# One VectorE addition at the end of a batch: step 2 of the block, or left to steps 6 and 7

## The chip, the cores and the metric

The kernel runs on one core of one Trainium2 chip. The metric is the device time of one execution in microseconds (us), lower is better. A timed result is the median of several executions; each execution also reports the mean clock that TensorE was granted, as a share of full speed.

Names of the engines: PE is TensorE (PEld its weight loads), DVE is VectorE, ACT is ScalarE, POOL is GpSimd. The whole span of a trace is 1.7 to 1.9 us shorter than the device time of the same execution.

## The reference, cut to what matters

```python
B, N, C = 4, 6208, 256
# attention over channels, one softmax matrix a (256 x 256) for each batch
qn = q / (norm(q over the N tokens) + 1e-6);  kn = the same of k
a = softmax(kn.T @ qn / tau)
x = v @ a
# channel mix of x with its own previous row
xk = mu_k * x + (1 - mu_k) * x_prev;  xr = mu_r * x + (1 - mu_r) * x_prev
out = sigmoid(xr @ w_r) * (relu(xk @ w_k) ** 2 @ w_v)      # d_ff = 1024
```

The matrix `a` of a batch needs sums over all its 6208 rows: the products k.T @ q (on PE) and the sums of squares of q and k. Only then can the rows of that batch go through the channel mix.

## The kernel before

Batch 0's sums are made first. Then come blocks `i` of 512 rows, 12 to a batch, each in 8 steps `j`. While the blocks of one batch run, the sums of the next batch are made in the gaps ("units"). So there are three batch ends inside the loop, of batches 1, 2 and 3. The first is at about 130 us.

The sums of squares: ScalarE squares 128 x 1024 elements into a tile, and an entry is put in the list `adds`. VectorE later adds the tile into `acc`, at steps that the loop chooses:

```python
def unit_square(b, g, s):
    ...
    elif (g, s) == (1, 0):
        t = pn.tile([P, 2, 2 * C], F32, name="acc", tag="acc", bufs=2)
        sums[b] = t                       # the first squares go straight into acc
    else:
        t = pq.tile([P, 2, 2 * C], F32, name="sq2", tag=f"f{s // 2}", bufs=6)
        adds.append((now[0] + 2, b, t))   # to be added two steps later at the earliest
    ...
def next_add():
    _, b, t = adds.pop(0)
    nc.vector.tensor_tensor(sums[b], sums[b], t, op=OP.add)          # L230
```

At a batch's end a chain of small pieces makes `a`, one piece a step. `fold` adds the two halves of the sums and waits until none of this batch's additions is left:

```python
return [evac, fold, None, None, norms, roots, pow2, None, invert, None, None,
        turn, exp, shares, None, weigh]
...
FOLD = 15
for i in ...:
    for j in range(8):
        ...                               # finish(): res of a finished part
        if chain:
            piece = chain[0]
            if len(chain) == FOLD and any(e[1] == holds[0] for e in adds):
                piece = None              # fold waits for the last addition
            else:
                chain.pop(0)
            if piece is not None:
                piece()
        ...                               # up(), square(), down(), mix(): the block's work
        if j in slots and pos["mm"] < len(units):
            unit()
        if adds and adds[0][0] <= now[0] and (j in (1, 6, 7)
                or j == 2 and adds[0][1] == holds[0] and chain):      # L766
            next_add()
        now[0] += 1
```

The block's work, as far as the argument needs it. `up` makes kT_ps on PE (L494), and ScalarE takes it out as `kr` (L499). `square` makes `kk = kr * kr` on VectorE (L512). `down` multiplies xr with w_r (L527) and kk with w_v (L531) into vr_ps on PE. vr_ps has two buffers; ScalarE (L540) and VectorE (L541) read it out into `res`, and the next L527 has to wait for that. kr has two buffers too.

Of the kernel before, what the change touches and what calls it, by code (L numbers as in the profile page):

```python
# [18 lines left out]
def kernel(  # L19
# [61 lines left out]
    adds = []  # L81
    sums = {}
    now = [0]
# [262 lines left out]
    def v_load(i):  # L346
        b, t = blocks[i]
        v_bf = p2.tile([P, S, C], BF16, name="v_bf", tag="v_bf", bufs=6)
        nc.gpsimd.dma_start(v_bf, v[b, t * M:(t + 1) * M, :].rearrange("(s p) c -> p s c", p=P))  # L349
        st[i, "v"] = v_bf  # L350
# [66 lines left out]
    def mix_first(key, a, dh):  # L417

        c = slice(a * H, (a + 1) * H)
        m = less[:, dh:dh + 1] if key == "xk" else less[:, 2 + dh:3 + dh]  # L420
        nc.vector.scalar_tensor_tensor(st[0, key][:, dh, c], st[0, "ps"][a][1][:, dh], m,
                                       st[0, "x"][:, dh, a * H + 1:(a + 1) * H + 1], op0=OP.mult, op1=OP.add)

    def up_first(fh, a):

        c = slice(a * H, (a + 1) * H)
        if (fh, a) == (0, 0):
            st[0, "kk"] = p2.tile([P, 8, M], BF16, name="kk", tag="kk", bufs=2)
            st[0, "kr", 0] = p2.tile([P, 4, M], BF16, name="kr", tag="kr", bufs=2)
        if a == 0:  # L430
            st[0, "kT", fh] = ps.tile([P, M], F32, name="kT_ps", tag="kT_ps", bufs=3)
        kT_ps = st[0, "kT", fh][:, c]
        for dh in range(2):
            nc.tensor.matmul(kT_ps, w_k_sb[:, dh, fh * P:(fh + 1) * P], st[0, "xk"][:, dh, c],
                             start=dh == 0, stop=dh == 1)
        nc.scalar.activation(st[0, "kr", 0][:, fh, c], kT_ps, AF.Relu, scale=0.5 ** 0.5)
# [50 lines left out]
    def up(i, fh):  # L487
        m = size(i)
        if fh == 0:
            st[i, "kk"] = p2.tile([P, 8, M], BF16, name="kk", tag="kk", bufs=2)  # L490
        xk = st[i, "xk"]
        kT_ps = ps.tile([P, M], F32, name="kT_ps", tag="kT_ps", bufs=3)
        for dh in range(2):
            nc.tensor.matmul(kT_ps[:, :m], w_k_sb[:, dh, fh * P:(fh + 1) * P], xk[:, dh, :m],  # L494
                             start=dh == 0, stop=dh == 1)
        if fh % 4 == 0 and (i or fh):
            st[i, "kr", fh // 4] = p2.tile([P, 4, M], BF16, name="kr", tag="kr", bufs=2)
        kr = st[i, "kr", fh // 4][:, fh % 4, :m]
        nc.scalar.activation(kr, kT_ps[:, :m], AF.Relu, scale=0.5 ** 0.5)  # L499
        if fh == 0 and by_act(i):  # L500
            nc.scalar.activation(st[i, "kk"][:, 0, :m], kr, AF.Square)
# [4 lines left out]
    def square(i, fh):  # L506
        m = size(i)
        n = 4 if fh < 4 and i < NBLK - 1 else 2
        if fh % n == n - 1:
            lo = 1 if fh == 3 and by_act(i) else fh % 4 + 1 - n  # L510
            kr = st[i, "kr", fh // 4][:, lo:fh % 4 + 1, :m]
            nc.vector.tensor_tensor(st[i, "kk"][:, fh // 4 * 4 + lo:fh + 1, :m], kr, kr, op=OP.mult)  # L512

    def down(i, j):

        s, h = divmod(j, 2)
        if s * P >= size(i) or i == NBLK - 1:
            return
        kk = st[i, "kk"]
        if j == 0:  # L520
            st[i, "res"] = p2.tile([P, S, D], F32, name="res", tag="res", bufs=3)
        if h == 0:
            vr_ps = ps.tile([P, 2 * D], F32, name="vr_ps", tag="vr_ps", bufs=2)
            st[i, "vr"] = vr_ps
            xr = st[i, "xr"]
            for dh in range(2):
                nc.tensor.matmul(vr_ps[:, D:], xr[:, dh, s * P:(s + 1) * P], w_r_sb[:, dh, :],  # L527
                                 start=dh == 0, stop=dh == 1)
        vr_ps = st[i, "vr"]
        for fh in (range(3) if h == 0 else range(3, 8)):  # L530
            nc.tensor.matmul(vr_ps[:, :D], kk[:, fh, s * P:(s + 1) * P], w_v_sb[:, fh, :],  # L531
                             start=fh == 0, stop=fh == 7)

    def finish(i, s):
        if i == NBLK - 1:
            return
        res = st[i, "res"]
        vr_ps = st[i, "vr"]

        nc.scalar.activation(res[:, s], vr_ps[:, D:], AF.Tanh, scale=0.5)  # L540
        nc.vector.scalar_tensor_tensor(res[:, s], res[:, s], 1.0, vr_ps[:, :D], op0=OP.add, op1=OP.mult)  # L541
        b, t = blocks[i]
        dst = out[b, t * M:(t + 1) * M, :].rearrange("(s p) c -> p s c", p=P)
        if i < NBLK - 2:
            if s == S - 1:
                nc.sync.dma_start(dst, res)
        elif s % 2:

            nc.sync.dma_start(dst[:, s - 1:s + 1], res[:, s - 1:s + 1])
# [82 lines left out]
    chain = []  # L632
    FOLD = 15
    holds = [0]
# [60 lines left out]
    for i in range(-2, NBLK - 1):  # L695
        for j in range(8):
            if j % 2:
                if j == 1 and i >= 1:
                    finish(i - 1, 3)
                elif j > 1 and i >= 0:  # L700
                    finish(i, j // 2 - 1)
            if j == 0 and 4 <= i + 6 < NBLK - 1:
                v_load(i + 6)
# [3 lines that stand above are left out]
                    piece = None  # L707
# [4 lines that stand above are left out]
            if i == -1 and j < 3:  # L712
                for fh, a in (((0, 0), (1, 0), (0, 1)), ((1, 1),), ())[j]:
                    up_first(fh, a)
                if j == 2:
                    up(0, 2)
            elif 0 <= i + 1 < NBLK:
                up(i + 1, j)
            if i >= 0:
                if j == 0 :  # L720
                    square(i, 7)
            if j > 0 and 0 <= i + 1 < NBLK:
                square(i + 1, j - 1)
            if j > 0 and i >= 0:
                down(i, j - 1)
            elif j == 0 and i >= 1:
                down(i - 1, 7)
            if 0 < i + 2 < NBLK:
                n = i + 2
                full = 0 < n < NBLK - 1  # L730
                if j in (0, 2) and full:
                    x_half(n, int(j > 0))
                if j == 3:
                    mix_delta(n)
                if j in (4, 5):
                    mix(n, "xk", int(j > 4))

            if j in (0, 2) and i == -1:
                for a in range(2):
                    mix_first("xr", a, int(j > 0))  # L740
            elif j in (0, 2) and 0 <= i + 1 < NBLK:
                mix(i + 1, "xr", int(j > 0))
            if (i, j) in ((-1, 6), (0, 4)):
                v_transpose_pe(i + 3, nc.vector.tensor_copy)()
            if j == 5 and 4 <= i + 5 < NBLK - 1:
                v_transpose(i + 5)
            if i == -1 and j in (5, 6):
                for u in early[:2] if j == 5 else early[2:]:
                    unit_matmul(*u)
            if (i, j) in ((0, 1), (0, 3)):  # L750
                unit_square(*early[j - 1])
            if i < 0:
                slots = ()
            elif i == 0:
                slots = (5, 6, 7)
            elif i < 7:
                slots = (1, 2, 3, 4, 5, 7) if i < 3 else (1, 2, 3, 4, 5, 6, 7)
            elif i == 7:
                slots = (1, 2, 7)
            elif (i - 7) % NB == 0:  # L760
                slots = (5, 7)
            else:
                slots = (1, 3, 4, 5, 7) if (i - 7) % NB in (1, 3, 6, 9) else (1, 3, 5, 7)
            if j in slots and pos["mm"] < len(units):
                unit()
            if adds and adds[0][0] <= now[0] and (j in (1, 6, 7) or j == 2 and adds[0][1] == holds[0] and chain):  # L766
                next_add()
            now[0] += 1
            if i >= 0 and i % NB == 2 and j == 1 and i // NB < B:
                left_go[0] = left_x(i // NB)  # L770
            if i >= 0 and i % NB == 4 and j == 4 and i // NB < B:
                left_go[0][0]()
            if i >= 0 and i % NB == 6 and j == 4 and i // NB < B:
                left_go[0][1]()
# [36 lines left out]
```

## Time and profile before

| | before |
|---|---|
| device time, median of 3 (range) | 511.45 us (511.42 to 511.74) |
| PE busy | 485.9 of 510.2 us, 95% |
| VectorE busy | 444.0 us, 87% |
| ScalarE busy | 446.3 us, 87% |
| the 69 additions into acc | 84.2 us, 1.220 us each |

The profile is that of a further execution, which took 512.12 us with a granted clock of 0.997.

The page of before, its first part (busy time and instructions of each engine), and from its fifth part the group of the additions:

```profile
PE 485.9 (95%) x3441; PEld 331.3 (65%) x3441; DVE 444.0 (87%) x751; ACT 446.3 (87%) x925; POOL 99.9 (20%) x146
...
L230 DVE TENSOR_TENSOR acc<-acc,sq 128x1024 f32<-128x1024 f32 x69 | 84.2, 1220 | 0.0
```

The 1.220 us of an addition agree with the Trainium skill, "VectorE: DVE Perf Modes", section "The TRN2 errata — SBUF-src ops pay a fixed extra latency per instruction": its formula (N + 151) / 0.96 ns for an fp32 tensor_tensor addition gives an estimate of 1224 ns at N = 1024. What counts for a busy queue is another number. From the start of an addition to the start of the next VectorE instruction the trace has 1.135 us, for the middle eight tenths of the 69 within 1 ns. Reported spans overlap a little, so this text adds up starts, not spans.

The waits of before (engine and line, what it waited for; us in total, times, longest):

```profile
PE vT_ps L365 <- DMA v_bf<-in_v_dram: 1.5, 1, 1.5
...
PE vr_ps L527 <- DVE res L541: 1.2, 2, 0.8
PEld L531 <- DVE kk L512: 1.1, 5, 0.3
```

After the start-up (some 45 us, in which it waits far more) PE waits little, and the wait of L527 for `res` is the one that the change aims at. Before's stretches show where it lies (length, then busy time of each engine with its number of instructions):

```profile
core 0: us, PE busy (x) PEld busy (x) DVE busy (x) ACT busy (x) POOL busy (x), PEclk, DMA share, GB/s
...
118.00:128.00 10.00, 10.00 (x77) 6.98 (x75) 9.50 (x16) 9.97 (x23) 2.52 (x4) 1.00 1.31 215
128.00:138.00 10.00, 8.82 (x66) 5.66 (x65) 10.00 (x15) 8.69 (x19) 0.00 (x0) 1.00 1.35 204
138.00:148.00 10.00, 10.00 (x75) 7.22 (x74) 9.93 (x19) 9.02 (x20) 3.36 (x4) 1.00 1.01 169
```

Of these stretches only in that from 128 to 138 us is PE not busy all the time, and there VectorE is busy all the time: at the first batch end the kernel is bound by VectorE for some 10 us. PE's timeline of before there (start, length, instruction, number of them, and in brackets the idle time ahead of it):

```profile
129.79 0.59 PE L494 MATMUL kT_ps<-xk,w_k_sb 128*128 128x512 bf16 x2
131.21 0.38 PE L527 MATMUL vr_ps<-w_r_sb,xr 128*128 128x256 bf16 x2 [0.83 <-DVE res L541]
...
133.67 0.38 PE L527 MATMUL vr_ps<-w_r_sb,xr 128*128 128x256 bf16 x2 [0.35 <-DVE res L541]
```

The brackets subtract a modelled end, which makes a wait look too short. By starts: the second of the two 512-column matmuls of 129.79 starts at 130.00, and the next matmul starts at 131.21, 1.21 us later. At full rate it would be 0.22 us later. PE has lost 0.99 us. That rate is the Trainium skill's, "TensorE: Matmul & The Clock Gate", section "Wait — 56ns, not 53.3ns?": N / 2.4 GHz plus about 2.5 ns, 216 ns for 512 columns; this trace agrees, with a pair of such matmuls every 0.43 us. In the same way before loses 0.51 us at 133.67, 0.13 at 136.40 and 0.09 at 148.61: together 1.72 us.

VectorE's timeline of before shows who is in the way:

```profile
129.61 1.22 DVE L230 TENSOR_TENSOR acc<-acc,sq 128x1024 f32<-128x1024 f32 x1
130.74 0.41 DVE L541 SCALAR_TENSOR_TENSOR res<-res,vr_ps 128x256 f32<-128x256 f32 x1
131.07 0.69 DVE L469 TENSOR_TENSOR delta<-xT 128x1024 bf16<-128x1024 bf16 x1
...
147.87 0.69 DVE L512 TENSOR_TENSOR kk<-kr 128x1024 bf16<-128x1024 bf16 x1
...
151.57 0.95 DVE L512 TENSOR_TENSOR kk<-kr 128x1536 bf16<-128x1536 bf16 x1
```

The addition of 129.61 is the one of step 2. It stands right ahead of the `res` of 130.74, for which PE waits.

### The profile page before, as it was taken

The numbers are of one execution on the slowest core, as the hardware profiler recorded it, in microseconds if no ns is written. First come the engines' busy times: TensorE is split into PE (matmuls) and PEld (weight loads), VectorE is DVE, ScalarE is ACT, GpSimd is POOL, SyncE is SP. The second block draws the span as 40 slices with busy tenths as digits, with TensorE's granted clock in tenths as the row PEclk, the third lists the DMA queues.
The fourth block names the chain that finished last, engine by engine and source line by source line (L and its number), as shares of the span: only waits on it lengthen the run. The fifth ranks groups of instructions, "written<-read, shape, count | busy, mean of one in ns | idle before, by whom it ended". The sixth has DMA issues, their size and how long they took to land. (4 is left out here: it accounts for less than half of the span.)

```text
span 510.2 us, 9336 instructions
## 1 busy us (share of the span) xinstructions
PE 485.9 (95%) x3441; PEld 331.3 (65%) x3441; DVE 444.0 (87%) x751; ACT 446.3 (87%) x925; POOL 99.9 (20%) x146
## 2 busy tenths in 40 slices
PE   4678999999999999999999999999999999999996
PEld 1345666766567677676666767667666666666675
DVE  3776899999999999999979999999878787878884
ACT  5767999999899999999899999999897888888784
POOL 0044342223054132221243133000131100000000
PEclk9998999999999999999999999999999999999999
DMA  8999999999989999997599999924497763333123
GB/s 330 409 299 201 191 173 199 143 192 199 201 153 198 180 205 172 171 184 134 102 157 227 173 173 177 176 74 116 84 178 137 143 106 97 93 85 83 45 81 104
DMA packets 133462, 83.46 MB, mean 164 GB/s; under 512 B 50660, under 2 KB 126760, under 8 KB 133416
## 3 DMA queue, kind: packets, MB, share of 16 engines
q0 software_dynamic: 56592, 33.01, 50.1%
q1 hardware_dynamic: 76504, 49.59, 41.1%
q8 instruction: 27, 0.44, 0.4%
q10 hardware_dynamic: 320, 0.26, 0.2%
q14 instruction: 19, 0.16, 0.1%
HBM read 78.71 MB, written 25.43 MB: 204 GB/s over the span
## 5 line engine op out<-in xcount | busy, mean ns | idle before, releaser
L499 ACT ACTIVATE kr<-kT_ps 128x512 bf16<-128x512 f32 (+1 forms) x390 | 232.0, 606 | 27.8 <-PE kT_ps L494 24.0
L531 PE MATMUL vr_ps<-w_v_sb,kk 128*128 128x256 bf16 x1536 | 231.0, 273 | 0.1
L494 PE MATMUL kT_ps<-xk,w_k_sb 128*128 128x512 bf16 (+1 forms) x780 | 230.0, 377 | 0.2 <-DVE xk L479 0.2
L531 PEld LDWEIGHTS <-kk 128*128 128x128 bf16 x1536 | 149.5, 98 | 58.9 <-DVE kk L512 1.1
L541 DVE SCALAR_TENSOR_TENSOR res<-res,vr_ps 128x256 f32<-128x256 f32 x192 | 80.1, 417 | 42.8 <-ACT res L540 42.8
L512 DVE TENSOR_TENSOR kk<-kr 128x1536 bf16<-128x1536 bf16 (+2 forms) x148 | 117.1, 791 | 0.2 <-ACT kr L499 0.2
L494 PEld LDWEIGHTS <-w_k_sb 128*128 128x128 bf16 x780 | 75.5, 98 | 27.5 <-issue 0.6
L230 DVE TENSOR_TENSOR acc<-acc,sq 128x1024 f32<-128x1024 f32 x69 | 84.2, 1220 | 0.0
L540 ACT ACTIVATE res<-vr_ps 128x256 f32<-128x256 f32 x192 | 76.5, 398 | 1.3 <-PE vr_ps L531 1.3
L527 PE MATMUL vr_ps<-w_r_sb,xr 128*128 128x256 bf16 x384 | 73.3, 272 | 1.2 <-DVE res L541 1.2
L479 DVE SCALAR_TENSOR_TENSOR xr<-delta,mu_t,xT 128x512 bf16<-128x512 bf16 x94 | 70.1, 746 | 0.0
L479 DVE SCALAR_TENSOR_TENSOR xk<-delta,mu_t,xT 128x512 bf16<-128x512 bf16 x94 | 70.1, 746 | 0.0
L527 PEld LDWEIGHTS <-xr 128*128 128x128 bf16 x384 | 37.6, 98 | 46.4 <-issue 2.6
L388 ACT CAST xT<-xT_ps 128x512 bf16<-128x512 f32 x94 | 55.4, 589 | 12.1 <-PE xT_ps L386 11.9
L386 PE MATMUL xT_ps<-vT,a_sb 128*128 128x512 bf16 x188 | 55.9, 379 | 0.9 <-DVE vT L371 0.8
L242 PE MATMUL s_ps<-qk 128*128 128x256 bf16 (+1 forms) x294 | 55.8, 273 | 0.0
L127 POOL DMA_DIRECT2D qk<-in_q_dram x39 | 26.2, 672 | 136.6 <-ACT kr L499 53.3
L226 ACT ACTIVATE sq<-qk 128x1024 f32<-128x1024 bf16 (+1 forms) x49 | 51.0, 1041 | 0.0
L349 POOL DMA_DIRECT2D v_bf<-in_v_dram x48 | 37.1, 776 | 50.7 <-DMA vT<-v_bf 32.4
L190 PE MATMUL s_ps<-qk 128*128 128x384 bf16 (+2 forms) x98 | 20.3, 352 | 16.0 <-ACT qk L147 14.9
L469 DVE TENSOR_TENSOR delta<-xT 128x1024 bf16<-128x1024 bf16 x47 | 32.3, 686 | 1.1 <-ACT xT L388 1.1
L242 PEld LDWEIGHTS <-qk 128*128 128x128 bf16 (+1 forms) x294 | 28.5, 98 | 5.6 <-issue 0.8
(105 smaller groups left out, 242.1 us busy)
## 6 DMA issues: line engine op xcount, KB each, us to landing
out_dram<-res SPq DMA_DIRECT2D x47, 512.0 KB, 4.2
v_bf<-in_v_dram POOLq DMA_DIRECT2D x48, 256.0 KB, 9.0
qk<-in_q_dram POOLq DMA_DIRECT2D x36, 256.0 KB, 8.0
qk<-in_k_dram POOLq DMA_DIRECT2D x36, 256.0 KB, 8.8
f<-in_q_dram SPq DMA_DIRECT2D x11, 512.0 KB, 9.4
f<-in_k_dram SPq DMA_DIRECT2D x11, 512.0 KB, 9.9
vT<-v_bf SPq DMA_TRANSPOSE x44, 6.7
f<-in_q_dram SPq DMA_DIRECT2D x2, 256.0 KB, 9.0
```

What stands on the lines that cost most here:

```text
L230: nc.vector.tensor_tensor(sums[b], sums[b], t, op=OP.add)
L242: nc.tensor.matmul(s_ps[:, ih, :], rows_at(qk, b, g, 0)[:rows, s, ih * P:(ih + 1) * P], rows_at(qk, b, g, 1)[:rows, s, :], start=t0 and ih ...
L386: nc.tensor.matmul(xT_ps, a_sb[:, b, ih, dh * P:(dh + 1) * P], vT[:, :, ih, :], start=ih == 0, stop=ih == 1)
L388: nc.scalar.copy(xT[:, dh, 1:], xT_ps)
L479: nc.vector.scalar_tensor_tensor(o[:, dh], st[i, "d"][:, dh], mu[:, dh:dh + 1], st[i, "x"][:, dh, :M], op0=OP.mult, op1=OP.add)
L494: nc.tensor.matmul(kT_ps[:, :m], w_k_sb[:, dh, fh * P:(fh + 1) * P], xk[:, dh, :m], start=dh == 0, stop=dh == 1)
L499: nc.scalar.activation(kr, kT_ps[:, :m], AF.Relu, scale=0.5 ** 0.5)
L512: nc.vector.tensor_tensor(st[i, "kk"][:, fh // 4 * 4 + lo:fh + 1, :m], kr, kr, op=OP.mult)
L527: nc.tensor.matmul(vr_ps[:, D:], xr[:, dh, s * P:(s + 1) * P], w_r_sb[:, dh, :], start=dh == 0, stop=dh == 1)
L531: nc.tensor.matmul(vr_ps[:, :D], kk[:, fh, s * P:(s + 1) * P], w_v_sb[:, fh, :], start=fh == 0, stop=fh == 7)
L540: nc.scalar.activation(res[:, s], vr_ps[:, D:], AF.Tanh, scale=0.5)
L541: nc.vector.scalar_tensor_tensor(res[:, s], res[:, s], 1.0, vr_ps[:, :D], op0=OP.add, op1=OP.mult)
```

## The change

The intent is to keep that addition out of the way of `res` and let it wait for steps 6 and 7.

```diff
-            if adds and adds[0][0] <= now[0] and (j in (1, 6, 7) or j == 2 and adds[0][1] == holds[0] and chain):
+            if adds and adds[0][0] <= now[0] and j in (1, 6, 7):
                 next_add()
```

In the built kernel no engine gains or loses an instruction. Only the first batch end is changed (batches 2 and 3 had no addition at step 2): one addition comes five steps later, so that additions now stand at both steps 6 and 7, and because `fold` waits for the last of them, the whole chain comes one step, about 1.2 us, later.

## The prediction

> What bounds the kernel now. The page gives PE 485.9 us busy of 510.2 (95%), granted clock 0.997, and the chain of waits that ended last lies on PE. The trace's PE starts show it harder: a pair of 128x512 matmuls starts every 0.43 us, which is the warm rate in the Trainium skill, "TensorE: Matmul & The Clock Gate", section "Wait — 56ns, not 53.3ns?" (N/2.4 GHz plus about 2.5 ns, 216 ns for 512 columns). Measured against that rate PE loses almost nothing from about 53 us on, except at one place: 131 to 137 us, where the first of the three batch ends falls. The waits view lists there PE vr_ps L527 <- DVE res L541, 2 times, 1.2 us. By starts: 0.99 us lost at 131.21, 0.51 at 133.67, 0.13 at 136.40, and 0.09 at 148.61 (kk of L512).
>
> What the change moves. Nothing is added or removed on any engine. On VectorE, comparing the built orders, one 128x1024 fp32 addition into acc (1.219 us median, 1.13 us from its start to the next) leaves its place before res L541 (at 129.61 us, step 2) and comes five steps later, so that two additions stand at steps 6 and 7. Because the fold waits for the last addition, the whole softmax chain of that batch (fold, norms, roots, inversion, transposes, exp, weighting) comes one step, about 1.2 us, later. The other two batch ends are unchanged: no addition stood at step 2 there.
>
> What it is worth. The removed addition sits directly before the res that PE waits for, so the intent is right: res (vr_ps of 131.21) starts at about 129.6 instead of 130.74, and the 0.99 us stall goes. But VectorE is busy without a gap from 118 us to 150 (timeline; 10.0 of 10.0 us in 128 to 138, 9.93 in 138 to 148), and its total work to the next kk is the same. I follow both queues:
> - 131.2: stall 0.99 goes. 133.7: 0.51 becomes about 0.37 (res starts near 132.08). 136.4: 0.13 stays. PE is now 1.13 us ahead.
> - The displaced addition then stands before the fold and kk L512 of fh 6 and 7, which still starts at 136.87 and ends at 137.55. PE now arrives 1.13 us plus the postponed norm matmuls (0.39 us) earlier, and must wait: a new stall of about 0.85 us on PEld L531 <- DVE kk. After the norm matmuls PE is about 0.3 us ahead.
> - At the next kk (147.87 to 148.55), which VectorE reaches at the same time as before, PE was already stalled by 0.09 us. It now waits about 0.39 us. The lead is gone.
> From there both queues have the same work. Sum: 1.72 us of stalls go, about 1.74 come. Net zero, within 0.2 us.
>
> Prediction: 511.4 us, range 511.0 to 511.9. Faster by over 2%: 0.005; within 2%: 0.99; slower: 0.005.
>
> What would show it. PE L527 <- DVE res falls from 1.2 us to about 0.5; PEld L531 <- DVE kk rises from 1.1 to about 2.2 us, with one wait near 0.85 at about 137.6 us and one near 0.4 at about 148.6. PE and DVE busy times stay. res of 130.74 starts near 129.6. Starts of PE after 150 us are shifted by less than 0.2 us.
>
> What would make it wrong. ScalarE, 87% busy, might hold VectorE: exp moves behind res and may delay kr and thus kk by 0.1 to 0.6 us near 151 us. If a VectorE gap opens between 130 and 148 us, PE loses up to that gap (slower by 0.3 to 0.6 us). If PE is let go earlier at kk than I think, up to 0.3 us stays as gain. Another chip may shift both times together.

## The result, and the profile after

| | before | after |
|---|---|---|
| device time, median of 4 | 511.44 us | 512.16 us |
| range | 510.46 to 511.74 | 511.43 to 513.28 |
| ratio, 95% interval | | 1.0019 (0.9996 to 1.0043) |

A ratio is the mean time of one kernel's runs over the mean of the other's of the same rounds, so it is not quite the ratio of the medians quoted. The median lies 0.3 us above the predicted range. That is two questions: what the trace says that the change costs, and what the rest of the 0.7 us is.

The page of after, its first part:

```profile
PE 482.2 (95%) x3382; PEld 331.1 (65%) x3441; DVE 444.4 (87%) x751; ACT 446.4 (88%) x925; POOL 100.7 (20%) x146
```

VectorE and ScalarE are as busy as before. PE has 3382 matmuls instead of 3441 only because 59 records are missing from this trace; the weight loads, 3441 in both, are complete. So PE's progress is compared by the starts of weight loads of the same number:

| weight load no. | 744 | 897 | 1075 | 3387 |
|---|---|---|---|---|
| before, us | 127.61 | 150.03 | 175.01 | 500.05 |
| after, us | 126.69 | 149.22 | 174.45 | 499.46 |
| after minus before, counted from no. 744 | 0 | +0.12 | +0.37 | +0.34 |

(Numbers count from 0.) Counting from no. 744, ahead of the moved addition, takes out the start-up, which differs between traces by up to 2.4 us with no difference in the code. (Here after's start-up was the shorter one, so 0.93 us are to be added to its times to compare them with before's.) The count must not start earlier: before loses 0.15 us at 126.95 us, ahead of the addition of 129.61, and the traces of no_add, pool_add and pe_add_warm below don't; counted from an earlier load, these 0.15 us would be put down to their edits. So the change costs about 0.3 us: 0.1 by 150 us, 0.25 more by 175, and nothing afterwards.

After's waits:

```profile
PEld L531 <- DVE kk L512: 2.8, 7, 1.1
...
PE vr_ps L531 <- DVE kk L512: 1.0, 2, 0.8
DVE kk L512 <- ACT kr L499: 0.6, 2, 0.4
PE vr_ps L527 <- DVE res L541: 0.2, 1, 0.2
```

L527's wait for `res` went from 1.2 to 0.2 us as intended, and L531's wait for `kk` came in its place, 2.8 us instead of 1.1. After's PE timeline:

```profile
131.61 0.38 PE L527 MATMUL vr_ps<-w_r_sb,xr 128*128 128x256 bf16 x2 [0.20 <-DVE res L541]
...
136.80 0.39 PE L531 MATMUL vr_ps<-w_v_sb,kk 128*128 128x256 bf16 x2 [0.78 <-DVE kk L512]
...
147.80 0.39 PE L531 MATMUL vr_ps<-w_v_sb,kk 128*128 128x256 bf16 x2 [0.22 <-DVE kk L512]
...
167.04 0.94 PE L531 MATMUL vr_ps<-w_v_sb,kk 128*128 128x256 bf16 x5
```

By starts, PE now loses 0.36 us at 131.61, 0.13 at 134.34, 0.95 at 136.80 and 0.39 at 147.80: 1.83 us instead of 1.72. That is +0.11, and the weight loads say +0.12. Then there is a loss that before does not have: the five matmuls of 167.04 take 0.94 us, while the same five take 0.71 us in before, because inside them one waits 0.22 us for `kk`. Before's line:

```profile
167.84 0.71 PE L531 MATMUL vr_ps<-w_v_sb,kk 128*128 128x256 bf16 x5
```

After's VectorE timeline, at the batch end and where the second part begins:

```profile
128.68 0.41 DVE L541 SCALAR_TENSOR_TENSOR res<-res,vr_ps 128x256 f32<-128x256 f32 x1
...
132.74 1.21 DVE L230 TENSOR_TENSOR acc<-acc,sq 128x1024 f32<-128x1024 f32 x1
133.87 0.41 DVE L541 SCALAR_TENSOR_TENSOR res<-res,vr_ps 128x256 f32<-128x256 f32 x1
134.21 1.21 DVE L230 TENSOR_TENSOR acc<-acc,sq 128x1024 f32<-128x1024 f32 x1
135.45 0.69 DVE L256 TENSOR_TENSOR sq<-acc 128x512 bf16<-128x512 f32 x1
...
147.06 0.68 DVE L512 TENSOR_TENSOR kk<-kr 128x1024 bf16<-128x1024 bf16 x1
...
150.97 0.96 DVE L512 TENSOR_TENSOR kk<-kr 128x1536 bf16<-128x1536 bf16 x1 [0.38 <-ACT kr L499]
```

The first `res` now starts at 128.68 (129.61 on before's time, where the addition stood), and two additions stand ahead of `fold` (L256). From there to the `kk` of 147.06 VectorE takes 147.06 − 128.68 = 18.38 us; before takes 147.87 − 129.61 = 18.26 us for the same instructions in another order. The 0.12 us are there. The visible part is between the second addition and the fold, which reads its result: 135.45 − 134.21 = 1.24 us, where every addition of before has 1.135.

At 150.97 VectorE waits 0.38 us for ScalarE's `kr`, which it did not do in before (its line of 151.57 above). ScalarE's timeline there, first before, then after:

```profile
148.36 0.46 ACT L315 ACTIVATE e_sb<-st_ps,rn 128x256 f32<-128x256 f32 x1
...
149.25 0.59 ACT L499 ACTIVATE kr<-kT_ps 128x512 bf16<-128x512 f32 x1
149.73 0.58 ACT L388 CAST xT<-xT_ps 128x512 bf16<-128x512 f32 x1
150.20 0.40 ACT L540 ACTIVATE res<-vr_ps 128x256 f32<-128x256 f32 x1
```

```profile
147.29 0.60 ACT L499 ACTIVATE kr<-kT_ps 128x512 bf16<-128x512 f32 x1
148.66 0.59 ACT L388 CAST xT<-xT_ps 128x512 bf16<-128x512 f32 x1 [0.78 <-PE xT_ps L386]
149.15 0.39 ACT L540 ACTIVATE res<-vr_ps 128x256 f32<-128x256 f32 x1
149.42 0.48 ACT L315 ACTIVATE e_sb<-st_ps,rn 128x256 f32<-128x256 f32 x1
...
150.32 0.61 ACT L499 ACTIVATE kr<-kT_ps 128x512 bf16<-128x512 f32 x1
```

In before the exponentials of the softmax (L315) run ahead of the copy of xT and of `res`. In after, one step later, ScalarE first idles 0.78 us for PE, and the exponentials run behind `res`, in front of the next `kr`. So this `kr` is late, VectorE waits for it, and the loss reaches PE when the two meet again, some 17 us later.

### The rest of the difference: two groups of times

In 28 runs of the kernel before on two chips (made for the experiments below), 14 took 509.45 to 510.36 us with a granted clock of 0.999 to 1.000, and 14 took 510.98 to 512.22 us with a clock of 0.996 or 0.997; none lies between. On the two later chips the split is less clean: one run of before took 510.83 us with a clock of 0.997 and one 512.00 us with 0.999, and the slowest took 515.91 us. The traces tell what the second group has. Before's trace (512.12 us, clock 0.997), then that of the experiment step3 (509.98 us, clock 1.000), between 40 and 44 us; the last columns are PEclk, DMA share and GB/s:

```profile
40.00:44.00 4.00, 3.61 (x23) 2.67 (x24) 1.13 (x5) 1.66 (x5) 1.08 (x2) 0.60 1.14 206
```

```profile
40.00:44.00 4.00, 3.55 (x29) 2.23 (x27) 3.16 (x11) 3.22 (x8) 1.35 (x3) 1.00 1.12 205
```

In before the clock is at half for one stretch of 3.41 us, from 39.76 us on. The Trainium skill, "TensorE: Matmul & The Clock Gate", section "What's actually happening", says that the clock is either full or half, decided over free-running windows of 3413 ns, and that an idle window halves it. The two states and the length agree with the traces. They do not show an idle window: in the 3.41 us ahead of the stretch PE was busy for 2.49 us in before, and for 70 to 79% of the time in the five traces that have such a stretch (much of it transposes and matmuls of one column). Nor is PE's wait of 1.5 us for a load of v (the first of the waits shown for before) the cause in general: after has the stretch, from 38.30 us on, without any such wait ahead of it. Every trace of a run with a clock of 0.996 or 0.997 has this stretch (before, before_again, after, after_again, pe_add_again: PEclk 0.57 to 0.79 here), and no trace with 0.998 or more has it. Why one execution falls into it and the next does not was not tested.

So a median of three or four runs says which group most of them fell in, to about 1.5 us. None of after's first four runs (clocks 0.992 to 0.997) is in the lower group; but of before's four runs three are in the upper one as well, and the fourth (510.46 us) lies between. So the groups alone do not explain the rest of the 0.7 us.

### The profile page after: what moved, and what is told of

It reads as the page before. It is cut to its first block, busy times and chain, and to the rows that moved or that the text cites. A ratio compares the mean times of both kernels' runs of the same rounds, so it can differ in the third digit from the quotient of the medians.

```text
span 509.7 us, 9277 instructions
## 1 busy us (share of the span) xinstructions
PE 482.2 (95%) x3382; PEld 331.1 (65%) x3441; DVE 444.4 (87%) x751; ACT 446.4 (88%) x925; POOL 100.7 (20%) x146
## 5 line engine op out<-in xcount | busy, mean ns | idle before, releaser
L531 PE MATMUL vr_ps<-w_v_sb,kk 128*128 128x256 bf16 x1536 | 231.4, 273 | 1.5 <-DVE kk L512 1.0
L494 PE MATMUL kT_ps<-xk,w_k_sb 128*128 128x512 bf16 (+1 forms) x722 | 217.6, 377 | 0.3 <-DVE xk L479 0.2
L531 PEld LDWEIGHTS <-kk 128*128 128x128 bf16 x1536 | 149.4, 98 | 60.5 <-DVE kk L512 2.8
L512 DVE TENSOR_TENSOR kk<-kr 128x1536 bf16<-128x1536 bf16 (+2 forms) x148 | 116.7, 789 | 0.6 <-ACT kr L499 0.6
L527 PE MATMUL vr_ps<-w_r_sb,xr 128*128 128x256 bf16 x384 | 73.3, 272 | 2.8 <-DVE res L541 0.2
L527 PEld LDWEIGHTS <-xr 128*128 128x128 bf16 x384 | 37.6, 98 | 45.2 <-issue 1.3
L386 PE MATMUL xT_ps<-vT,a_sb 128*128 128x512 bf16 x188 | 55.9, 379 | 0.9 <-DVE vT L371 0.8
```

The source lines that it names most:

```text
L386: nc.tensor.matmul(xT_ps, a_sb[:, b, ih, dh * P:(dh + 1) * P], vT[:, :, ih, :], start=ih == 0, stop=ih == 1)
L494: nc.tensor.matmul(kT_ps[:, :m], w_k_sb[:, dh, fh * P:(fh + 1) * P], xk[:, dh, :m], start=dh == 0, stop=dh == 1)
L512: nc.vector.tensor_tensor(st[i, "kk"][:, fh // 4 * 4 + lo:fh + 1, :m], kr, kr, op=OP.mult)
L527: nc.tensor.matmul(vr_ps[:, D:], xr[:, dh, s * P:(s + 1) * P], w_r_sb[:, dh, :], start=dh == 0, stop=dh == 1)
L531: nc.tensor.matmul(vr_ps[:, :D], kk[:, fh, s * P:(s + 1) * P], w_v_sb[:, fh, :], start=fh == 0, stop=fh == 7)
```

## The experiments

Theories. **A**: the chain one step later costs, because its pieces (above all the exponentials) meet the block's work on ScalarE at a worse place. **N**: noise; the change costs nothing. **B**: the displaced addition costs by its new place, ahead of fold. **C**: what matters is the place ahead of `res`: an addition costs there, and without one there the time is won. Any other letters are explained where they stand. Timed results are 6 runs of a kernel against 11 of before on the same chip unless said otherwise. The noise between two runs is larger than what is sought; the weight-load starts repeat to 0.04 us or better between traces of one kernel. The table collects them as difference from before, counted from load no. 744. Its last column is VectorE's time for the batch end: from where the addition of 129.61 us stands in before (or where the next instruction stands in its place) to the `kk` of 147.87 us.

| kernel | by 150 us | by 175 us | by 500 us | VectorE, us |
|---|---|---|---|---|
| before | 0 | 0 | 0 | 18.26 |
| before_again | −0.01 | −0.01 | −0.03 | 18.26 |
| after | +0.12 | +0.37 | +0.34 | 18.38 |
| after_again | +0.12 | +0.36 | +0.30 | 18.38 |
| norms_back | +0.12 | +0.12 | +0.10 | 18.38 |
| chain_late | −0.00 | +0.25 | +0.23 | 18.26 |
| step3 | −0.01 | −0.01 | −0.04 | 18.26 |
| no_add | −1.28 | −1.28 | −1.31 | 17.12 |
| pool_add | +0.58 | +0.58 | +0.55 | 18.96 |
| exp_early | +0.12 | +0.12 | +0.07 | 18.39 |
| both_back | +0.16 | +0.16 | +0.11 | 18.43 |
| pe_add | −1.04 | −1.04 | −1.08 | 17.14 |
| pe_add_again | −1.03 | −1.03 | −1.05 | 17.14 |
| pe_add_warm | −1.16 | −1.16 | −1.21 | 17.14 |

Up to 150 us PE loses what VectorE's time grows, to within 0.02 us, with two corrections. In no_add, pool_add and pe_add_warm VectorE is already 0.12 us further ahead of PE at load no. 744 than in the other traces, since PE had waited near 102 or 113.6 us; with that no_add is −1.16 us against VectorE's −1.14, pool_add +0.70 against +0.70, and pe_add_warm −1.04 as pe_add. And the pe_add kernels gain 0.09 us less than VectorE saves; they also give PE 8 more matmuls, which take 0.20 us.

(For the three pe_add kernels the 8 weight loads that they add are counted off, and the 4 of pe_add_warm's extra start-up matmuls.)

### after_again and before_again: both kernels once more

The files are unchanged copies of after and of before.

> The changed kernel again, five rounds. In the first two traces PE, followed instruction by instruction, is 0.91 us ahead of before at 60 us (start-up), 0.81 ahead at the second kk (148.6 us of before) and 0.56 ahead from 169 us on: a real cost of about 0.35 us. Theory A (VectorE's total work up to the second kk decides, so the stalls only change places; then exp, one step later, holds ScalarE and VectorE and makes a new kk stall of 0.22 us near 167.6): again +0.3 to +0.4 us from 60 us to the end in the trace, stalls of about 0.36, 0.13, 0.95 and 0.39 us at 131.6, 134.3, 136.8 and 147.8, one of 0.2 near 167.6; timed +0.2 to +0.6 us. Rival N (only noise of the start-up): +0.0 in both within 0.1 us in the trace and no stall near 167.6.

> The kernel before against itself, to show the noise: ratio 1.000 with an interval of about 0.001 to each side. In its trace the same stalls as before (0.99, 0.51, 0.13 and 0.09 us near 131, 134, 136 and 149); the start-up until 45 us may differ by up to 1 us, PE from 60 us to the end by under 0.1 us.

On one chip after took 511.18 us (510.25 to 512.42), before_again 511.15 (509.91 to 511.79), and the shared runs of before 510.36 (509.63 to 511.97). The ratios are 1.001 (0.9991 to 1.0029) and 1.000 (0.9981 to 1.0018). The medians of the two files that are the same differ by 0.8 us, so a median says nothing here about 0.3 us. The traces do: before_again lies on before within 0.03 us, and after_again repeats after (+0.36 by 175 us), with the same stalls by starts (0.365, 0.128, 0.948, 0.382 and 0.221 us). N falls as an account of the trace, and it may account for the other half of the 0.7 us, which no run shows.

### norms_back: the late fold, but the rest of the chain in its old step

On the kernel after, one of the empty steps of batch 1's chain is taken out:

```diff
-        return [evac, fold, None, None, norms, roots, ...]
+        return [evac, fold] + [None] * (1 if b == 1 else 2) + [norms, roots, ...]
...
-                if len(chain) == FOLD and any(...):
+                if len(chain) == FOLD - (holds[0] == 1) and any(...):
```

> The change, but with one empty step fewer between fold and norms of that batch: the addition stands displaced, the softmax chain from the norms on stands where it stood before. Theory A: no stall near 167.6, PE from 60 us to the end within +0.15 us of before (against +0.35 for the change); the kk stall near 136.8 is smaller by the 0.39 us of the norm matmuls (about 0.55), the one near 148 larger or equal; sum unchanged there. Rival B (the displaced addition itself costs the 0.35 us, by two additions in a row before kk): +0.35 us as for the change.

510.58 us against 510.36, ratio 1.0001 (0.9983 to 1.0019). In the trace the 0.22 us near 167 us are gone, and the +0.12 by 150 us is still there. The norms' matmuls now come too early for the fold, as PE's timeline of norms_back shows:

```profile
135.48 0.25 PE L263 MATMUL bank<-ones,sq 128*128 128x1 bf16 x4 [0.76 <-DVE sq L256]
```

This wait (0.87 us by starts) stands in the place of the wait of 0.95 us for `kk`. So A explains the second part of the loss (+0.25), and not the first. The first, +0.12, is what is left of B, which had expected the whole 0.35 us here.

### chain_late: only the chain later, the addition where it was

On the kernel before, one empty step is put in:

```diff
-        return [evac, fold, None, None, norms, roots, ...]
+        return [evac, fold] + [None] * (3 if b == 1 else 2) + [norms, roots, ...]
...
-                if len(chain) == FOLD and any(...):
+                if len(chain) == FOLD + (holds[0] == 1) and any(...):
```

> The kernel before, addition in its old place, but one empty step more between fold and norms of that batch: only the chain moves by one step. Theory A: the old stalls 0.99, 0.51 and 0.13 us stay, ScalarE idles near 148.5 us as in the change, a kk stall of about 0.2 us comes near 167.6 to 168.5; PE from 60 us to the end +0.2 to +0.35 us. Rival B: +0.0 us, no such stall.

510.92 us against 510.36, ratio 1.0003 (0.9985 to 1.0022). The weight loads: nothing by 150 us, +0.25 by 175. The timeline of chain_late, VectorE's line and PE's, shows after's wait and after's loss, with the addition in its old place:

```profile
149.41 0.96 DVE L512 TENSOR_TENSOR kk<-kr 128x1536 bf16<-128x1536 bf16 x1 [0.38 <-ACT kr L499]
...
165.49 0.94 PE L531 MATMUL vr_ps<-w_v_sb,kk 128*128 128x256 bf16 x5
```

The late chain alone makes the second part, and norms_back without it loses it: A is shown for the +0.25.

### step3: the addition one step later, behind the `res` that PE waits for

On the kernel before:

```diff
-            if ... (j in (1, 6, 7) or j == 2 and adds[0][1] == holds[0] and chain):
+            if ... (j in (1, 6, 7) or j == 3 and adds[0][1] == holds[0] and chain):
```

> The kernel before with the addition one step later (step 3, behind res and delta, before kk), the chain unmoved. Theory A (the sum of VectorE work counts, not its place): the stall of 0.99 us at 131.2 goes, the one of 0.51 at 133.7 grows to about 1.45 us; PE from 60 us to the end within 0.1 us of before. Rival C (the place ahead of the res that PE waits for is what costs): about 1.0 us faster.

511.10 us against 510.31 (another chip), ratio 1.0011 (0.9991 to 1.0031); four of its six runs were in the upper group. PE's timeline of step3:

```profile
131.65 0.38 PE L527 MATMUL vr_ps<-w_r_sb,xr 128*128 128x256 bf16 x2 [1.33 <-DVE res L541]
```

The first wait (0.99 us) is gone, and the second is 1.49 us by starts, where before has 0.99 + 0.51 = 1.50. The sum is −0.01 us by 150 us. The place of the addition is worth nothing: moved past one `res` it is paid at the next. C falls in its second half.

### no_add: the addition left out (its result is wrong)

On the kernel before, at step 2:

```diff
-    def next_add():
+    def next_add(drop=False):
         _, b, t = adds.pop(0)
-        nc.vector.tensor_tensor(sums[b], sums[b], t, op=OP.add)
+        if not drop:
+            nc.vector.tensor_tensor(sums[b], sums[b], t, op=OP.add)
...
-                next_add()
+                next_add(j == 2)
```

> The kernel before without that one addition (wrong on purpose: two rows per partition of one group miss in batch 1's norms), chain unmoved. Theory A: VectorE has 1.13 us less to do up to 149 us and the stalls 0.99 and 0.51 fall to 0 and about 0.37, the one at 136.4 stays 0.13; at both kk no new wait, because both queues are ahead by the same 1.1 us: 1.0 to 1.3 us faster from 60 us to the end, timed 0.9 to 1.4. If the give-back were caused by something other than VectorE's work (rival D, ScalarE or a PSUM buffer): under 0.5 us faster.

The result lacks one tile of squares (the comparison's tolerance passed it all the same). 509.58 us against 510.31, ratio 0.9982 (0.9961 to 1.0004). The trace has −1.28 us by 150 us, and it is kept to the end: PE's losses fall from 1.72 to 0.44 us (0.23 + 0.13 + 0.08). About 0.12 us of it is the lead that VectorE had from PE's earlier wait, so some 1.16 us are the edit's. This is the largest gain that any place for this addition could have. It is won by taking 1.135 us of VectorE's queue away, not by moving them.

### pool_add: the same addition, at the same step, on GpSimd

On the kernel before:

```diff
-        nc.vector.tensor_tensor(sums[b], sums[b], t, op=OP.add)
+        (nc.gpsimd if pool else nc.vector).tensor_tensor(sums[b], sums[b], t, op=OP.add)
...
-                next_add()
+                next_add(j == 2)
```

> The kernel before with that one addition on GpSimd, which idles from about 125 to 140 us there (15.58 us before its pow). If GpSimd does it in under 5 us without slowing VectorE: as without the addition, 1.0 to 1.3 us faster than before from 60 us to the end and right results, so faster than both kernels. If the two engines disturb each other, VectorE's instructions between 129 and 134 us show longer spans and the gain is smaller or negative.

512.42 us against 510.31, ratio 1.0048 (1.0020 to 1.0075); one run took 516.49. By the trace it loses 0.58 us at the batch end, 0.70 without the lead of VectorE. Its timeline there, GpSimd's line and VectorE's:

```profile
128.39 2.73 POOL L230 TENSOR_TENSOR acc<-acc,sq 128x1024 f32<-128x1024 f32 x1 [10.63 <-ACT xT L388]
...
129.15 2.52 DVE L469 TENSOR_TENSOR delta<-xT 128x1024 bf16<-128x1024 bf16 x1
```

GpSimd's addition takes 2.73 us, and VectorE's `delta` beside it 2.52 us instead of 0.69. PE then waits 2.08 us at one place. The Trainium skill, "GPSIMD Engine Reference", section "1. Specifications", says that the two engines share their SBUF interfaces and that VectorE instructions with two SBUF inputs contend with GpSimd; this trace agrees, and shows that here the contention costs VectorE more (1.83 us) than the addition that was taken from it (1.135 us).

The trace's 0.58 us are not all of the timed 2 us. The same trace has waits of 0.39 us near 102 us and 0.93 us near 113.6 us ahead of xT_ps (L386), before the place of the edit. no_add (0.95 us) and pe_add_warm (0.31 and 1.44 us) have such waits too. vT, which L386 reads, is brought by a transposing DMA; that this is their cause was not tested.

### exp_early: the late chain, with only the exponentials a step earlier

On the kernel after, for batch 1 `turn` and `exp` share one step:

```diff
+        def turn_exp():
+            turn()
+            exp()
+
+        last = [turn_exp, None] if b == 1 else [turn, exp]
-        return [evac, ..., None, None, turn, exp, shares, None, weigh]
+        return [evac, ..., None, None] + last + [shares, None, weigh]
```

> The changed kernel with exp of that batch issued in the step of its transposes, one step earlier, so that on ScalarE it stands ahead of the kr and the xT copy again, as before the change; norms, inversion, transposes and weighting stay one step late. Theory A (exp behind the xT copy leaves ScalarE idle 0.78 us first and makes it late afterwards): the kk stall near 167.6 us goes; PE from 60 us to the end +0.1 us against before, not +0.2 to +0.35. If another part of the late chain (weighting, inversion) makes that stall: it stays at 0.22.

510.23 us against 510.83 (a third chip, on which one run of before took 515.91), ratio 0.9982 (0.9948 to 1.0016). The trace: +0.12 by 150 us and by 175, so the second part is gone. The timeline of exp_early, VectorE's line and PE's (its lines are 5 further down; its L517 and L536 are L512 and L531):

```profile
149.04 0.95 DVE L517 TENSOR_TENSOR kk<-kr 128x1536 bf16<-128x1536 bf16 x1
...
165.56 0.71 PE L536 MATMUL vr_ps<-w_v_sb,kk 128*128 128x256 bf16 x5
```

`kk` no longer waits for `kr`, and the five matmuls take 0.71 us as in before. Of the late chain it is the exponentials on ScalarE that cost the +0.25. The late matmuls and VectorE pieces do not.

### both_back: the rest of the +0.12

On the kernel after, batch 1's chain gets a pause ahead of the fold, so that the fold no longer follows the addition whose result it reads, and is shortened further on:

```diff
+        if b == 1:
+            return [evac, None, fold, None, norms, roots, pow2, invert, None, None, turn, exp, shares, None, weigh]
...
-                if len(chain) == FOLD and any(...):
+                if len(chain) == FOLD - (holds[0] == 1) and any(...):
```

> The addition displaced as in the change, but the fold one step later still (so it does not stand directly behind the addition whose result it reads, where 1.24 us instead of 1.13 pass from start to start) and the chain from the inversion on at its old place. Theory A: both terms, +0.11 us (addition then fold) and +0.25 us (late exp), go: PE from 60 us to the end within 0.06 us of before, although the stalls still stand at other places (new: the norms wait about 0.6 us for the fold). Rival B (displaced addition costs): +0.1 us or more stays by 150 us.

510.78 us against 510.83, ratio 0.999 (0.9953 to 1.0027). The trace has +0.16 by 150 us, nothing more after. The gap ahead of the fold did go (from the addition to the next instruction 1.135 us again), but from the first scaling of s_sb in `invert` to the next instruction it now takes 0.44 us instead of 0.27. VectorE's sum is 18.43 us, no better than after's 18.38. The edit removed one delay (0.11 us) and made another (0.17), and PE's loss followed the sum. What makes the scaling longer was not looked into.

So the +0.12 is VectorE's own time, and the gap ahead of the fold is nearly all of it. The fold follows directly on its last addition in four traces (after, after_again, norms_back, exp_early), with 1.247 to 1.252 us from start to start; VectorE's sum there is 18.38 to 18.39 us, and PE loses 0.12 in each. In before, step3 and chain_late the fold does not follow directly, the sum is 18.26, and PE loses nothing. That the reading of the result makes the gap was not tested by an edit, but the start-up of before shows the same: an addition of L162 takes 0.319 to 0.327 us from start to start where the next instruction reads its result (nine times), and 0.210 where it does not (once). In each of these nine, as ahead of the fold, the reader starts 34 or 35 ns after the reported end, while other instructions start before it.

### pe_add and pe_add_again: the addition left to the norms' matmuls

no_add's lesson is that the VectorE queue must lose work. The norms are column sums made on PE from the folded squares, and a matmul adds up rows as it runs. So on the kernel after one tile of batch 1's squares is not added at all; the norms' matmuls read it, by 8 more of one column each:

```diff
             sums[b] = t
+        elif (b, g, s) == (1, NB, 0):
+            t = sums[b, "extra"] = pn.tile([P, 2, 2 * C], BF16, name="sqx", tag="sqx", bufs=1)
         else:
...
-            for t, rows in ((sums.pop((b, "left"))[:, 0], L), (sums.pop(b), P)):
+            parts = [(sums.pop((b, "left"))[:, 0], L), (sums.pop(b), P)]
+            if (b, "extra") in sums:
+                extra = sums.pop((b, "extra"))
+                parts[1:1] = [(extra[:, 0], P), (extra[:, 1], P)]
+            for n, (t, rows) in enumerate(parts):
...
```

> Right results, meant to beat both: that one tile of squares is written in bf16 and summed by 8 more norm matmuls on PE instead of by the VectorE addition; chain as before. Theory A: VectorE has 1.13 us less to do, stalls 0.99 and 0.51 become 0 and about 0.25 as without the addition (there 1.5 us were gained, apart from one DMA wait of 0.95), and PE pays about 0.3 us: 1.0 to 1.3 us faster than before from 60 us to the end. If VectorE's work were not what counts: +0.3 us slower.

> The version with the tile of squares summed on PE once more, on another call: theory A, from just before the change's place to the end 1.1 us less than before in the trace; timed 1.0 to 2.0 us faster (0.996 to 0.998), as the first run's 0.9949 was helped by slow runs of before (up to 515.91). If the first run was luck of the start-up: no difference.

The result is correct. On the third chip pe_add took 508.92 us (508.44 to 509.14) against 510.83, ratio 0.9949 (0.9917 to 0.9981). On a fourth it took 510.51 us (509.10 to 513.90) against 510.61, ratio 1.0006 (0.9977 to 1.0034). The traces agree: −1.04 and −1.03 us, kept to the end, with only 0.36 and 0.13 us lost at the batch end. PE's timeline of pe_add:

```profile
134.30 0.35 PE L269 MATMUL bank<-ones,sqx 128*128 128x1 bf16 x8
```

A gain of 1.04 us would be a ratio of about 0.998 (1 − 1.04/511), and both intervals hold it. Whether pe_add beats both kernels in time stays open: once it clearly did, once it did not.

### pe_add_warm: pe_add, and more matmuls to keep the clock up

```diff
     exp()
+    keep_warm(4)
     v_transpose_pe(1, nc.scalar.copy)()
```

> The same with four more dummy matmuls in the gap of PE near 39 us. The times of all kernels so far fall into two groups 1.5 us apart, and the upper group has the granted clock 0.996 to 0.997 where the lower has 0.999 to 1.000; in the traces the upper group has 3.41 us at half clock near 40 us, after PE's idle 1.5 us there. If the idle gap causes the half clock, no or fewer runs show 0.997 and the median falls by 0.5 to 1 us more; if not, the two groups stay as they are.

509.11 us (508.33 to 510.98) against 510.83, ratio 0.9961 (0.9926 to 0.9996). None of its six runs had a clock of 0.996 or 0.997, but on this chip neither had pe_add without the extra matmuls (0.998 to 1.000). The experiment tells nothing about the cause of the two groups. (Its text speaks of an idle 1.5 us ahead of the half clock; of the five traces with the half clock only that of before has it.)

## Why the prediction was right or wrong

- **What bounds the kernel at the batch end: right.** VectorE's queue does. (Its "without a gap from 118 us" overlooks 0.50 us of idle time ahead of 119.54 us, which does not matter here.) step3 and no_add show it from two sides: moving the addition is worth −0.01 us, taking it away −1.28 (some 1.16 of it the edit's).
- **131 to 134 us: right.** Predicted: the 0.99 us goes, 0.51 becomes about 0.37, 0.13 stays. Measured 0.36 and 0.13. `res` started where it was predicted (129.61 on before's time).
- **The new stalls at kk: right.** Predicted about 0.85 us near 137.6 and 0.39 near 148.6; measured 0.95 and 0.39 us, at 137.7 and 148.7 on before's time. The sum by 150 us was predicted as 1.72 going and 1.74 coming, and is 1.72 against 1.83. The first term that was mis-sized is VectorE's own: it takes 18.38 us instead of 18.26 for the same instructions. Nearly all of that is seen as 1.247 us instead of 1.135 from an addition to the fold that reads its result. The prediction took 1.13 for every addition.
- **"From there both queues have the same work. Sum: 1.72 us of stalls go, about 1.74 come. Net zero, within 0.2 us": wrong.** This is the step that failed. ScalarE did not have the same order: the exponentials moved behind `res` and ahead of a `kr`. VectorE waits 0.38 us for that, and PE loses 0.22 us at 167.6 us. The weight-load starts are late by 0.37 us at 175 us and by 0.34 at 500. chain_late makes this part alone (+0.25), and norms_back and exp_early take it away. The prediction had named it as what would make it wrong ("might delay kr and thus kk by 0.1 to 0.6 us near 151 us") and put it at zero in the sum. A second check of the prediction, "Starts of PE after 150 us are shifted by less than 0.2 us", fell with it.
- **The views: right in kind, off in size.** L527's wait for `res` fell to 0.2 us in the waits (predicted 0.5; by starts it is 0.36 + 0.13 = 0.49), and the weight loads' wait for `kk` rose to 2.8 us (predicted 2.2).
- **"Range 511.0 to 511.9": wrong.** The real cost, +0.3 us, would have fitted (511.45 + 0.34 = 511.8), and so would the noise without it (512.16 − 0.34 = 511.8); together they did not. The range was drawn around three runs within 0.3 us of each other. They lay in one group of runs; the kernel before itself takes 509.45 to 512.22 us on two chips, in two groups about 1.5 us apart, and up to 515.91 us on a third. Of the 0.7 us between the medians the trace accounts for about 0.3. The rest is within what the same kernel does from run to run (the two copies of before on one chip: 510.36 and 511.15 us). It was not shown which run-to-run cause made it.

Still open: what makes the scaling in both_back longer, why some executions get the half-clock stretch, what causes the waits near 102 and 113.6 us, and whether pe_add wins in time.

## What to carry to other kernels

Where an engine is busy without a gap over several waits, moving an instruction inside that stretch only moves the wait: here 1.14 us less waiting for `res` (1.63 to 0.49) came back as 1.25 us more waiting for `kk` (0.09 to 1.34). Ask what leaves that engine's queue, and check what each piece that moves along meets on every other engine, since a late piece on ScalarE cost more than the addition's new place. Before predicting tenths of a microsecond, learn the spread of the baseline over many runs, and compare kernels by starts of the same instruction in their traces, counted from just ahead of the change.

## What the Trainium skill lacked or had wrong

- "VectorE: DVE Perf Modes" says in its section "The DRAIN you can't avoid" that a semaphore after each instruction costs nothing extra (measured there on eight copies), and gives no cost for an instruction that reads the result of the one right before it. Here an fp32 128x1024 addition holds the queue for 1.135 us, and for 1.247 to 1.252 us where the next instruction reads its result (four traces).
- The same page's errata formula gives the reported length (1224 ns, measured 1220), but what a saturated queue pays from start to start is shorter, 1135 ns. The section cited here does not tell the two apart.
- "TensorE: Matmul & The Clock Gate", section "What's actually happening", gives the half clock as what follows at least one idle window of about 3.4 us. In the five traces here that have a half-clock stretch near 40 us, PE was busy for 70 to 79% of the 3.41 us before it. Part of that time went to transposes and matmuls of one column; whether these count as idle no run here tests. The traces with the stretch are of executions with a mean clock of 0.996 or 0.997, which on two chips marks the upper of two groups of times of one kernel, 509.45 to 510.36 and 510.98 to 512.22 us.
